# Neighborhood attention on one core: a rebuilt start, a new order of filler work, and a ring for the edge columns

## The chip, the core and the metric

The kernel runs on one core of a Trainium2 chip. The metric is the device time of one execution in microseconds. The engines are TensorE (PE; PEld is its weight load), VectorE (DVE), ScalarE (ACT), GpSimd (POOL) and SyncE (SP), which here only issues DMAs.

## The reference

Every pixel of a 224 x 224 image with 192 channels attends to a 7 x 7 neighborhood with dilation 2, clipped at the border; one head, all 192 channels.

```python
qkv = x @ wqkv                                 # q, k, v of 192 channels
r0 = jnp.clip(ir - 6, 0, H - 1 - 12); c0 = jnp.clip(ic - 6, 0, W - 1 - 12)
nidx = (r0 + 2*a) * W + (c0 + 2*b)             # a, b = 0..6: 49 neighbors
logits = jnp.einsum('bnc,bnkc->bnk', q, k[nidx]) * C ** -0.5
o = jnp.einsum('bnk,bnkc->bnc', softmax(logits), v[nidx]) @ wo
```

## The kernel before

Dilation 2 splits the keys by the parity of rows (rc) and of columns (cc). A step (rc, j) handles eight query rows of each column parity; j runs to 14, so there are 28 steps. In a step, order lists eight ticks: four for cc 0 and four for cc 1, each with three or four key tiles n of 8 rows x 8 columns from two neighboring key blocks, 128 keys.

Weights are folded. AW holds q times k weights, so that g = AW x is scored against raw x; WP folds v and output weights. The tile xt[b] is the block of 16 image rows with channels on partitions; XN[rc] has pixels on partitions, and between its channel columns stands a field of group columns (one-hot), from which the softmax sum comes. XA and XB are the key operands, copied from xt (key_items: "first" on GpSimd, "second" on VectorE), with one-hot key rows and columns in the spare rows of XB; GB carries the mask in the same rows on the query side.

In each tick s_stage (L364) does the score matmuls and ScalarE the exp; y_stage (L388) of the tick before multiplies the probabilities with XN; y_evac (L407) copies a finished half of y to SBUF, one tile on ScalarE and one on VectorE. Between them filler items are popped from one list: g_piece (L315), six a step, which makes the query side for the next step, and o_item (L419), seven a step, which makes the output of the step before: four matmuls, a reciprocal and a multiplication on VectorE. Both use the PSUM pool ps_go, which has two buffers. The list goes g, o, g, o, ... The g_piece of kind 1 is copied by VectorE (L333) and ScalarE (L334).

Near the image's left and right edge the clipped windows need other rows: gather_edges (L279) copies six columns of xt on GpSimd, edge_item multiplies them, and g_edges (L338) puts the results into g's first columns with eight small GpSimd copies a step, at tick 0 of the step before.

All instructions run on each engine in the order in which the program writes them (manual_schedule, L55). The loads of XN for later steps are divided between GpSimd's queue (nine tiles) and SP's (five); SP also issues the transposing load of xt (load_xt, L63, at tick 1 of a step with rc 0) and the stores of a finished step (store, L436).

The start (L472 to L521) loads both halves of XN, from SP, GpSimd and, behind the AW products, ScalarE (L486). It turns two blocks into xt with 84 TensorE transposes (L500), copied by ScalarE and VectorE, then makes keys, edges and the six g pieces of step 0, spreads masks and one-hot rows by DMA inside SBUF, and last makes the value weights.

Of the kernel before, what the change touches and what calls it, by code (L numbers as in the profile page):

```python
# [26 lines left out]
def kernel(  # L27
# [45 lines left out]
    nc.scalar.dma_start(out=w_lo[:], in_=wqkv[0:128, :])  # L73
    nc.scalar.dma_start(out=w_hi[:], in_=wqkv[128:192, :])
    nc.scalar.dma_start(out=wo_lo[:], in_=wo[0:128, :])
    nc.scalar.dma_start(out=wo_hi[:], in_=wo[128:192, :])

# [6 lines left out]
    def xn_items(rc, m, eng):  # L84
        if not (0 <= m < NJ):
            return []
        res = []
        r0, p0 = 16 * m + rc, (m % 2) * 64
        for n in range(NT):
            def one(n=n):  # L90
                eng.dma_start(out=XN[rc][p0:p0 + 64, XP * n + 64:XP * (n + 1)],  # L91
                              in_=xp[r0: r0 + 15: 2, TW * n: TW * (n + 1), :])
            res.append(one)
        return res
# [4 lines left out]

    run(xn_items(0, 0, nc.sync))  # L100
    run(xn_items(0, 1, nc.gpsimd))
    run(xn_items(1, 0, nc.sync))
# [4 lines left out]
    def turn_weights(X):  # L107
        for (dt_, d0, dn) in ((wT_lo, 0, 128), (wT_hi, 128, 64)):
            tp = ps_y.tile([128, 2, 128], BF, name="tp_w", tag="y")
# [8 lines left out]
    for nm in wnames:  # L118
        AW[nm] = const.tile([128, 128], BF, name="aw_" + nm)
        nc.vector.memset(AW[nm][:], 0.0)  # L120
# [9 lines left out]
    def make_aw():  # L130
        for k_, (reg, us) in enumerate(uses.items()):
# [5 lines left out]
            for (nm, o0, o1, d0) in us:  # L137
                nc.scalar.mul(AW[nm][rows, d0:d0 + o1 - o0], pt[rows, o0:o1], scale)
# [5 lines left out]

    def make_wp():
        for (cc, kt, c0, cn, p0) in ((0, 0, 64, 128, 0), (0, 1, 0, 64, 64), (1, 0, 0, 128, 0), (1, 1, 128, 64, 0)):
            pt = ps_y.tile([128, 512], F32, name="prW", tag="y")
            nc.tensor.matmul(pt[p0:p0 + cn, 0:C], lhsT=wT_lo[:, 2, c0:c0 + cn], rhs=wo_lo[:], start=True, stop=False)
            nc.tensor.matmul(pt[p0:p0 + cn, 0:C], lhsT=wT_hi[:, 2, c0:c0 + cn], rhs=wo_hi[:], start=False, stop=True)
            nc.scalar.copy(out=WP[p0:p0 + cn, cc, kt, 0:C], in_=pt[p0:p0 + cn, 0:C])  # L150

# [101 lines left out]
    def fill_groups(rc):  # L253
        t = XN[rc]
        nc.gpsimd.tensor_copy(out=t[:, 0:NT * XP].rearrange("p (n c) -> p n c", c=XP)[:, :, 0:64],
                              in_=grp[:].unsqueeze(1).to_broadcast([128, NT, 64]))
        nc.gpsimd.tensor_copy(out=t[:, NT * XP:], in_=grp[:])

# [19 lines left out]
    ge = {}  # L278
# [8 lines left out]
    def edge_item(b):  # L287
# [27 lines left out]
    def g_piece(rc, j, kind, ra):  # L315
# [5 lines left out]
        for (r0, n_, b, l0) in step_rows(rc, j):  # L321
# [5 lines left out]
            for i, (w, k) in enumerate(ws):  # L327
                nc.tensor.matmul(pg[:, a_ - ra:b_ - ra, p0:p0 + S - 3], lhsT=AW[w][:], rhs=xt[b][:, k, la:lb:2, p0:p0 + S - 3],  # L328
# [35 lines left out]
    def s_stage(st, cc, ns):  # L364
# [15 lines left out]
        nc.scalar.activation(out=G.p[:, 0:off], in_=s_ps[:, 0:off], func=ACTF.Exp)  # L380
# [7 lines left out]
    def y_stage(G):  # L388
        st, cc = G.st, G.cc
        xn = XN[st.rc]  # L390
        for (n, a, b, off) in G.sub:
            c0 = XP * n + (128 if cc == 0 else 256)
            c1 = XP * n + (0 if cc == 0 else 384)
            w = b - a
            pv = G.p[:, off:off + BR * w].rearrange("p (r c) -> p r c", c=w)
            for h in range(2):
# [5 lines left out]
                for kt, l0 in ((0, c0), (1, c1)):  # L402
                    nc.tensor.matmul(ys[kt][:, :, a_ - h0:b_ - h0], lhsT=xn[:, l0:l0 + 128], rhs=pv[:, :, a_ - a:b_ - a],  # L403
# [14 lines left out]

    def o_item(st, t):  # L419
        if t == 0:  # L420
            st.o = work.tile([128, NO, 2, C], BF, name="o_all", tag="o_all", bufs=2)
        po = ps_go.tile([128, 2, 256], F32, name="po", tag="go")
        for cc in range(2):
            for kt in range(2):
                nc.tensor.matmul(po[:, cc, 0:C + 1], lhsT=st.ysb[cc][:, kt, t, :], rhs=WP[:, cc, kt, :], start=(kt == 0), stop=(kt == 1))  # L425
        rs = work.tile([128, 2, 1], F32, name="rs", tag="rs", bufs=4)
        nc.vector.reciprocal(out=rs[:], in_=po[:, :, C:C + 1])  # L427
        if st is steps[-1]:
            nc.vector.tensor_scalar(out=st.o[:, t, 0, :], in0=po[:, 0, 0:C], scalar1=rs[:, 0, :], scalar2=None, op0=ALU.mult)
            nc.scalar.mul(st.o[:, t, 1, :], po[:, 1, 0:C], rs[:, 1, :])  # L430
        else:
            nc.vector.tensor_tensor(out=st.o[:, t], in0=po[:, :, 0:C], in1=rs[:].to_broadcast([128, 2, C]), op=ALU.mult)  # L432
        if t == NO - 1:
            store(st)

    def store(st):  # L436
        o = st.o
        runs = _affine([16 * b + l0 + 2 * i for (r0, n_, b, l0) in step_rows(st.rc, st.j) for i in range(n_)])
        last = st is steps[-1]
        for k, (i0, n_, d0, stp) in enumerate(runs):  # L440
# [6 lines left out]
            else:  # L447
                e = slice(NI * i0, NI * (i0 + n_ - 1) + 1, NI)
                for i in range(n_):
                    p0 = NI * (i0 + i)  # L450
                    (nc.sync, nc.scalar)[i % 2 if last else 0].dma_start(
                        out=op[d0 + i * stp, NO - 3:S - 3, :].rearrange("(i t) c -> i (t c)", t=NO),
                        in_=o[p0 + 1:p0 + NI].rearrange("p t two c -> p (t two c)"))
            q = nc.scalar if last and k else nc.sync
            q.dma_start(out=op[dr, NO - 4, :], in_=o[e, NO - 1].rearrange("p two c -> p (two c)"))
            q.dma_start(out=op[dr, 0:3, C:2 * C], in_=o[e, 0:3, 0, :])
            q.dma_start(out=op[dr, 0:3, 0:C], in_=o[e, 3:6, 0, :])
            q.dma_start(out=out[0][dr, W - 6:W, :], in_=o[e, 0:6, 1, :])
# [3 lines left out]
    last_of = {(0, 1): [(0, 0)], (0, 3): [(0, 1)], (1, 6): [(1, 1)], (1, 7): [(1, 0)]}  # L462
# [13 lines left out]
    cols_iota(1)  # L476
    make_groups()
# [3 lines left out]
    onehot_keys()  # L481
    mask_cols(1)
    turn_weights(0)
    turn_weights(1)
    make_aw()
    run(xn_items(1, 1, nc.scalar))  # L486
    spread_rows(nc.sync, 0, 1)
    spread_keys(nc.sync, 1, 0)
    fill_groups(0)
    fill_groups(1)  # L490
    for b in range(2):
        new_xt(b)
    for rc in range(2):
        for k in range(3):
            for h in range(2):
                hn = NT // 2
                tp = ps_y.tile([128, hn, 2, BR, TW], BF, name="tp_x", tag="y")
                for n in range(hn):
                    c0 = XP * (hn * h + n) + 64 + 128 * k
                    nc.tensor.transpose(tp[:, n].rearrange("p b r c -> p (b r c)"), XN[rc][:, c0:c0 + 128], ident[:])  # L500
                for b in range(2):
                    (nc.scalar.copy if b == h else nc.vector.tensor_copy)(  # L502
                        out=xt[b][:, k, rc:16:2, HALF * h:HALF * h + HALF].rearrange("p r (n c) -> p n r c", c=TW), in_=tp[:, :, b])
        ki = [key_items(b, rc) for b in range(2)]
        for i in range(4):
            ki[0][i]()
            ki[1][i]()
    for b in range(2):
        gather_edges(b)
        edge_item(b)  # L510
    run(g_items(0, 0))
    g_edges(0, 0)
    for gi in range(1, NG):
        mask_row(gi)
    spread_cols(nc.sync, 0)
    spread_keys(nc.sync, 0, 1)
    spread_cols(nc.sync, 1)
    spread_rows(nc.sync, 1, NG)
    spread_keys(nc.sync, 1, 1)
    turn_weights(2)  # L520
    make_wp()  # L521
# [3 lines left out]
    for si, st in enumerate(steps):  # L525
        st.ysb = [work.tile([128, 2, NO, 128], BF, name=f"ysb{cc}", tag=f"ysb{cc}", bufs=2) for cc in range(2)]
        nx = steps[si + 1] if si + 1 < len(steps) else None
        g_q = g_items(nx.rc, nx.j) if nx else []
        if si > 1:
# [3 lines left out]
        fill = []  # L533
        while g_q or o_q:
            fill += g_q[:1] + o_q[:1]
            g_q, o_q = g_q[1:], o_q[1:]
        fill = fill[::-1]
        for ti, (cc, ns) in enumerate(order):
            G = s_stage(st, cc, ns)
            if ti == 0 and nx:  # L540
                g_edges(nx.rc, nx.j)
            if fill and (ti > 0 or nx):
                fill.pop()()
            if prev is not None:
                y_stage(prev)
                for key in last_of.get((prev.cc, prev.tick), []):
                    y_evac(prev.st, *key)
# [10 lines left out]
            if fill and len(fill) >= len(order) - 1 - ti:  # L558
                fill.pop()()
            if ti == 4 and st.rc == 1:  # L560
                gather_edges(st.j + 2)
# [59 lines left out]
```

## Time and profile before

| | us |
|---|---|
| median of 3 runs | 422.8 (422.27 to 423.28) |
| profiled execution | 426.73 |
| its span | 424.8 |
| PE busy | 342.4 (81%) |
| DVE busy | 277.0 (65%) |
| ACT busy | 250.0 (59%) |
| POOL busy | 245.7 (58%) |

The span runs from the first to the last instruction of the profiled execution; its time has something around the span. Busy shares are means over the start, the middle and the end.

### The profile page before, as it was taken

The numbers are of one execution on the slowest core, as the hardware profiler recorded it, in microseconds if no ns is written. First come the engines' busy times: TensorE is split into PE (matmuls) and PEld (weight loads), VectorE is DVE, ScalarE is ACT, GpSimd is POOL, SyncE is SP. The second block draws the span as 40 slices with busy tenths as digits, with TensorE's granted clock in tenths as the row PEclk, the third lists the DMA queues.
The fourth block names the chain that finished last, engine by engine and source line by source line (L and its number), as shares of the span: only waits on it lengthen the run. The fifth ranks groups of instructions, "written<-read, shape, count | busy, mean of one in ns | idle before, by whom it ended". The sixth has DMA issues, their size and how long they took to land.

```text
span 424.8 us, 12956 instructions
## 1 busy us (share of the span) xinstructions
PE 342.4 (81%) x5012; PEld 288.5 (68%) x5012; DVE 277.0 (65%) x680; ACT 250.0 (59%) x557; POOL 245.7 (58%) x567
## 2 busy tenths in 40 slices
PE   5233899877898889998889878898898889898970
PEld 2123478766777778777778757787777778777850
DVE  2617437664777777676777657777777777777770
ACT  5023486662767666667666656666666575767650
POOL 9416500843885757776658866757858675790000
PEclk9999999996999999999999999999999999999996
DMA  5350090494895959979595995969869597542223
GB/s 148 104 140 3 2 178 2 108 167 120 168 203 125 170 155 189 159 147 188 154 175 143 153 192 137 168 148 194 179 134 174 160 159 167 141 128 72 66 67 65
DMA packets 96723, 57.86 MB, mean 136 GB/s; under 512 B 78134, under 2 KB 91270, under 8 KB 96662
## 3 DMA queue, kind: packets, MB, share of 16 engines
q1 hardware_dynamic: 84025, 44.42, 53.4%
q0 software_dynamic: 11040, 11.38, 12.6%
q10 hardware_dynamic: 1597, 1.24, 1.1%
q8 instruction: 39, 0.64, 0.7%
q14 instruction: 22, 0.18, 0.1%
HBM read 19.56 MB, written 19.27 MB: 91 GB/s over the span
## 4 chain that ended last, share of the span: by engine, by line
PE 44%; DVE 19%; ACT 18%; DMA 8%; issue 4%; SPq 3%; POOL 1%; ACTq 0%; DVEq 0%; POOLq 0%
PE pg L328 15%; PE po L425 10%; PE y L403 8%; DVE gbt L333 7%; ACT gbt L334 6%; DVE o_all L432 6%; DMA xn<-in_x_dram 6%; PE s_ps L376 5%; ACT p_sb L380 5%; PE s_ps L375 4%; ACT ysb L417 3%; SPq L91 2%; ACT ga L331 2%; DVE xb L272 2%; DVE rs L427 1%
## 5 line engine op out<-in xcount | busy, mean ns | idle before, releaser
L380 ACT ACTIVATE p_sb<-s_ps 128x448 bf16<-128x448 f32 x224 | 109.6, 489 | 87.9 <-PE s_ps L376 69.2
L91 POOL DMA_DIRECT2D xn<-in_x_dram x230 | 127.8, 592 | 35.6 <-PE y L403 21.3
L425 PE MATMUL po<-WP,ysb 128*128 128x193 bf16 x784 | 104.4, 250 | 23.2 <-ACT ysb L417 18.6
L403 PE MATMUL y<-p_sb,xn 128*128 128x112 bf16 (+2 forms) x1736 | 113.7, 207 | 7.8 <-DMA xn<-in_x_dram 7.1
L403 PEld LDWEIGHTS <-xn 128*128 128x128 bf16 x1736 | 97.9, 98 | 27.1 <-DMA xn<-in_x_dram 8.2
L432 DVE TENSOR_TENSOR o_all<-po,rs 128x384 bf16<-128x384 f32 x189 | 105.4, 558 | 8.4 <-DVE rs L427 0.2
L375 PE MATMUL s_ps<-ga,xa 128*128 128x112 bf16 (+2 forms) x812 | 104.4, 211 | 0.0
L376 PE MATMUL s_ps<-gbt,xb 128*128 128x112 bf16 (+2 forms) x812 | 101.9, 211 | 1.8 <-DVE xb L272 0.2
L425 PEld LDWEIGHTS <-ysb 128*128 128x128 bf16 x784 | 59.3, 98 | 34.2 <-ACT ysb L417 24.5
L376 PEld LDWEIGHTS <-xb 128*128 128x128 bf16 x812 | 77.3, 98 | 4.1 <-DVE xb L272 3.9
L417 DVE CAST ysb<-y 128x448 bf16<-128x448 f32 x104 | 64.0, 616 | 21.9 <-PE y L403 21.0
L375 PEld LDWEIGHTS <-xa 128*128 128x128 bf16 x812 | 77.7, 98 | 0.4 <-issue 0.4
L427 DVE RECIPROCAL rs<-po 128x2 f32<-128x2 f32 x196 | 32.6, 166 | 63.8 <-PE po L425 60.3
L268 POOL COPY xa<-xt 128x896 bf16<-128x896 bf16 x56 | 52.0, 977 | 17.8 <-DVE xt L502 17.8
L345 POOL COPY ga<-ge 128x9 bf16<-128x9 bf16 (+1 forms) x112 | 28.5, 276 | 53.6 <-DVE ge L301 50.2
L417 ACT CAST ysb<-y 128x448 bf16<-128x448 f32 x104 | 56.1, 540 | 0.6
L334 ACT CAST gbt<-pg 64x424 bf16<-64x424 f32 x56 | 28.4, 507 | 37.6 <-DVE gbt L333 37.6
L333 DVE CAST gbt<-pg 64x436 bf16<-64x436 f32 x56 | 33.8, 603 | 15.5 <-PE pg L328 14.7
L328 PE MATMUL pg<-xt,aw_m 128*128 128x327 bf16 (+2 forms) x252 | 42.5, 298 | 0.0
L328 PE MATMUL pg<-xt,aw_o 128*128 128x109 bf16 (+2 forms) x168 | 30.4, 290 | 10.7 <-ACT gbt L334 8.0
L331 ACT CAST ga<-pg 128x436 bf16<-128x436 f32 x56 | 29.4, 525 | 5.5 <-PE pg L328 5.5
L345 POOL COPY gbt<-ge 64x9 bf16<-64x9 bf16 (+1 forms) x112 | 29.9, 267 | 3.2
(91 smaller groups left out, 267.7 us busy)
## 6 DMA issues: line engine op xcount, KB each, us to landing
out_dram<-o_all SPq DMA_DIRECT2D x26, 630.0 KB
xn<-in_x_dram POOLq DMA_DIRECT2D x230, 48.0 KB, 4.4
xn<-in_x_dram SPq DMA_DIRECT2D x148, 48.0 KB
out_dram<-o_all SPq DMA_DIRECT2D x13, 78.8 KB
gbt<-gbt SPq DMA_DIRECT2D x3, 280.0 KB
out_dram<-o_all SPq DMA_DIRECT2D x52, 9.0 KB
xn<-in_x_dram ACTq DMA_DIRECT2D x14, 48.0 KB
xb<-xb SPq DMA_DIRECT2D x3, 224.0 KB
```

Source lines behind the costliest of these rows:

```text
L91: eng.dma_start(out=XN[rc][p0:p0 + 64, XP * n + 64:XP * (n + 1)], in_=xp[r0: r0 + 15: 2, TW * n: TW * (n + 1), :])
L328: nc.tensor.matmul(pg[:, a_ - ra:b_ - ra, p0:p0 + S - 3], lhsT=AW[w][:], rhs=xt[b][:, k, la:lb:2, p0:p0 + S - 3], start=(i == 0), stop=(i ...
L333: nc.vector.tensor_copy(out=Bt[0][0:64, ra:rb, 3:S], in_=pg[0:64, :, 0:S - 3])
L334: nc.scalar.copy(out=Bt[1][64:128, ra:rb, 6:S], in_=pg[64:128, :, 3:S - 3])
L345: nc.gpsimd.tensor_copy(out=dst.rearrange("p r s -> p s r"), in_=src)
L375: nc.tensor.matmul(o, lhsT=XA[:, cc, st.rc, n, :], rhs=A[cc][:, :, a:b], start=True, stop=False)
L376: nc.tensor.matmul(o, lhsT=XB[:, cc, st.rc, n, :], rhs=Bt[cc][:, :, a:b], start=False, stop=True)
L380: nc.scalar.activation(out=G.p[:, 0:off], in_=s_ps[:, 0:off], func=ACTF.Exp)
L403: nc.tensor.matmul(ys[kt][:, :, a_ - h0:b_ - h0], lhsT=xn[:, l0:l0 + 128], rhs=pv[:, :, a_ - a:b_ - a], start=not ys[2 + kt], stop=True, s ...
L417: eng(out=dst, in_=src.rearrange("p r i t -> p t i r"))
L425: nc.tensor.matmul(po[:, cc, 0:C + 1], lhsT=st.ysb[cc][:, kt, t, :], rhs=WP[:, cc, kt, :], start=(kt == 0), stop=(kt == 1))
L432: nc.vector.tensor_tensor(out=st.o[:, t], in0=po[:, :, 0:C], in1=rs[:].to_broadcast([128, 2, C]), op=ALU.mult)
```

## The change

Start: the four weight loads are written further down. Only the first key block is loaded at once (rc 0 from SP, rc 1 from GpSimd), and load_xt(1) stands behind it on SP. The transposes take 64 partitions and fill xt[0] alone, left half first; they now stand ahead of the mask work. Step 0 uses 64 keys (kp) and starts with other tiles (first_order); the two g pieces of kind 2, the keys of rc 1, the value weights and the second edge item become its filler. The second block's XN of rc 1 is loaded by SP. Group columns are written by VectorE, twice per tile (XP 448 to 512). Half of the AW scalings go to VectorE, and seven matmuls on constant data ("warm") are written in.

Steps: the list becomes g, g, o, o, g, o, o, ...; surplus items are popped later; SP's list of loads is emptied ahead of load_xt; edge_item moves to tick 1 of a step with rc 0, g_edges to tick 3, gather_edges to the end of a step with rc 1. The edge results lie in two rings of 24 rows (one per row parity), so that a step's rows are mostly one run of copies.

End: the last step's outputs of cc 0 are made within it, two tiles at a time (o_pair), those of cc 1 behind it in four buffers, on VectorE and ScalarE in turn; its stores go over three queues.

```diff
-XP = 448
+XP = 512
-    run(xn_items(0, 1, nc.gpsimd))
-    run(xn_items(1, 0, nc.sync))
+    run(xn_items(1, 0, nc.gpsimd))
+    load_xt(1)
...
+    ge = [const.tile([128, 15, NE], BF, name=f"ge{cl}") for cl in range(2)]      # NE = 3 * BR
+        for cl in range(2):                                       # edge_item
+            for (i, p, n_) in ring_runs(cl, BR * b, BR):
+                nc.vector.tensor_copy(out=ge[cl][:, :, p:p + n_], in_=pg[:, :, 2 * i + cl:2 * (i + n_ - 1) + cl + 1:2])
...
+    def o_pair(st, cc, t, pool, tag, k):
+        n_ = min(2, NO - t)
+        po = pool.tile([128, 2, 256], F32, name="po", tag=tag)
+        for i in range(n_):
+            o_mm(po[:, i, 0:C + 1], st, cc, t + i)
+        nc.vector.reciprocal(out=rs[:, 0:n_], in_=po[:, 0:n_, C:C + 1])
+        if k % 2 == 0:
+            nc.vector.tensor_tensor(out=st.o[:, t:t + n_, cc, :], ...)
+        else:
+            for i in range(n_):
+                nc.scalar.mul(st.o[:, t + i, cc, :], po[:, i, 0:C], rs[:, i, :])
...
+    new_xt(0)
+    for h in range(2):
+        for rc in range(2):
+            for k in range(3):
+                for n in range(hn):
+                    nc.tensor.transpose(..., XN[rc][0:64, c0:c0 + 128], ident[0:64, 0:64])
+                (nc.vector.tensor_copy if h == 0 and (k + rc) % 2 else nc.scalar.copy)(out=xt[0][...], in_=tp[:])
+    make_groups() ... onehot_keys(); fill_groups(0)
+    run(k00[0:2]); gather_edges(0)
+    g_piece(0, 0, 0, 0); g_piece(0, 0, 1, 0); g_piece(0, 0, 0, 4)
+    warm(4); g_piece(0, 0, 1, 4); warm(3)
+    edge_item(0); g_edges(0, 0)
...
+        return [lambda: g_piece(0, 0, 2, 0), lambda: g_piece(0, 0, 2, 4), f4, fw] + wp + g1[:3] + [f6] + g1[3:]
...
+            fill = g_q[:2]
+            if nx is None:
+                o_q += [(lambda k=k: o_pair(st, 0, 2 * k, ps_go, "go", 0)) for k in range((NO + 1) // 2)]
+            while g_q or o_q:
+                fill += o_q[:2] + g_q[:1]
...
             if ti == 1 and st.rc == 0:
+                run(sp_q)
+                sp_q = []
                 load_xt(st.j + 2)
...
-            if fill and len(fill) >= len(order) - 1 - ti:
+            if si > 0 and st.rc == 0 and ti == 1 and st.j + 1 < NJ:
+                edge_item(st.j + 1)
+            if si > 0 and ti == 3 and nx:
+                g_edges(nx.rc, nx.j)
+            if fill and (len(fill) >= nt - ti or (nx is None and ti < 4)):
                 fill.pop(0)()
```

## Rows read from the trace of the kernel before

**Rows 1.** The page, busy us, share of the span and instructions of the engines:

```profile
PE 342.4 (81%) x5012; PEld 288.5 (68%) x5012; DVE 277.0 (65%) x680; ACT 250.0 (59%) x557; POOL 245.7 (58%) x567
```

**Rows 2.** Windows: stretch, its us, busy us of each engine, granted clock, DMA share, GB/s:

```profile
28.00:52.20 24.20, 15.58 (x113) 10.71 (x113) 14.40 (x29) 9.94 (x24) 14.54 (x36) 0.98 0.07 17
...
150.00:200.00 50.00, 45.08 (x693) 38.64 (x692) 36.48 (x91) 32.84 (x72) 35.29 (x79) 1.00 0.88 165
```

**Rows 3.** Timeline of the start: start us, us, engine, line, operation [idle before, releaser]:

```profile
0.74 18.28 SPq L91 DMA_DIRECT2D xn<-in_x_dram  x28
...
9.89 0.28 DVE L251 TENSOR_SCALAR grp<-gi__189 128x64 bf16<-128x64 f32 x1 [6.81 <-POOL gi__189 L247]
...
11.74 2.34 PE L500 MATMUL tp_x<-ident,xn 128*128 128x128 bf16 x17 [0.42 <-DMA xn<-in_x_dram]
...
14.81 12.39 ACTq L91 DMA_DIRECT2D xn<-in_x_dram  x14
15.41 1.09 DVE L194 COPY xb<-t_r 32x1792 bf16<-32x1792 bf16 x1
...
27.24 0.53 ACT L502 COPY xt<-tp_x 128x448 bf16<-128x448 bf16 x1 [17.37 <-DMA gbt<-gbt]
...
48.94 2.78 DVE L230 CAST gbt<-rm 32x896 bf16<-32x896 f32 x5
...
52.20 0.28 PE L375 MATMUL s_ps<-ga,xa 128*128 128x112 bf16 x1
```

**Rows 4.** Timeline of ScalarE: first exps of steps 1 and 27, one same tick two steps apart:

```profile
62.62 0.54 ACT L380 ACTIVATE p_sb<-s_ps 128x448 bf16<-128x448 f32 x1
...
146.83 0.45 ACT L380 ACTIVATE p_sb<-s_ps 128x336 bf16<-128x336 f32 x1 [0.79 <-PE s_ps L376]
...
172.09 0.45 ACT L380 ACTIVATE p_sb<-s_ps 128x336 bf16<-128x336 f32 x1 [0.79 <-PE s_ps L376]
...
399.20 0.56 ACT L380 ACTIVATE p_sb<-s_ps 128x448 bf16<-128x448 f32 x1
```

**Rows 5.** Timeline of one step, from 385.98 us, TensorE's waits and a g evacuation:

```profile
388.39 0.34 PE L425 MATMUL po<-WP,ysb 128*128 128x193 bf16 x2 [0.71 <-ACT ysb L417]
...
389.62 0.60 DVE L333 CAST gbt<-pg 64x436 bf16<-64x436 f32 x1
...
390.26 0.51 ACT L334 CAST gbt<-pg 64x424 bf16<-64x424 f32 x1 [0.69 <-DVE gbt L333]
...
395.77 0.54 PE L328 MATMUL pg<-xt,aw_o 128*128 128x109 bf16 x4 [0.33 <-ACT gbt L334]
```

**Rows 6.** The page, costliest groups: busy us, mean ns, idle before and its releaser:

```profile
L432 DVE TENSOR_TENSOR o_all<-po,rs 128x384 bf16<-128x384 f32 x189 | 105.4, 558 | 8.4 <-DVE rs L427 0.2
...
L427 DVE RECIPROCAL rs<-po 128x2 f32<-128x2 f32 x196 | 32.6, 166 | 63.8 <-PE po L425 60.3
...
L417 ACT CAST ysb<-y 128x448 bf16<-128x448 f32 x104 | 56.1, 540 | 0.6
```

**Rows 7.** Timeline, TensorE's two long waits for x tiles:

```profile
98.31 0.37 PE L403 MATMUL y<-p_sb,xn 128*128 128x112 bf16 x2 [4.59 <-DMA xn<-in_x_dram]
...
253.40 0.27 PE L403 MATMUL y<-p_sb,xn 128*128 128x112 bf16 x2 [1.78 <-DMA xn<-in_x_dram]
```

**Rows 8.** Timeline of SP's queue over two steps:

```profile
110.38 7.83 SPq L66 DMA_TRANSPOSE xt<-in_x_dram  x1
118.31 3.46 SPq L91 DMA_DIRECT2D xn<-in_x_dram  x5
...
126.42 3.46 SPq L91 DMA_DIRECT2D xn<-in_x_dram  x5
131.02 0.92 SPq L445 DMA_DIRECT2D out_dram<-o_all  x1
```

**Rows 9.** Timeline of the end: the last normalization and the last stores:

```profile
415.15 0.42 ACT L430 ACTIVATE o_all<-po,rs 128x192 bf16<-128x192 f32 x1 [0.84 <-DVE o_all L429]
...
420.36 1.13 SPq L451 DMA_DIRECT2D out_dram<-o_all  x2
```

More of the change, by code (lines that the diff above doesn't have):

```diff
@@ L117 @@
     AW = {}
[L118 to L120 removed]
+    aw = const.tile([128, len(wnames), 128], BF, name="aw")
+    nc.vector.memset(aw[:], 0.0)
+    for i_, nm in enumerate(wnames):
+        AW[nm] = aw[:, i_, :]
     LO, HI = (0, 128, 0), (128, 64, 0)
@@ L476 @@
     cols_iota(1)
+    turn_weights(0, ps_y, "y")
+    turn_weights(1, ps_y, "y")
+    make_aw()
+    new_xt(0)
+    hn = NT // 2
+    for h in range(2):
+        for rc in range(2):
+            for k in range(3):
+                tp = ps_y.tile([128, hn, BR, TW], BF, name="tp_x", tag="y")
+                for n in range(hn):
+                    c0 = XP * (hn * h + n) + 128 + 128 * k
+                    nc.tensor.transpose(tp[:, n].rearrange("p r c -> p (r c)"), XN[rc][0:64, c0:c0 + 128], ident[0:64, 0:64])
+                (nc.vector.tensor_copy if h == 0 and (k + rc) % 2 else nc.scalar.copy)(
+                    out=xt[0][:, k, rc:16:2, HALF * h:HALF * h + HALF].rearrange("p r (n c) -> p n r c", c=TW), in_=tp[:])
     make_groups()
@@ L481, with warm @@
     onehot_keys()
+    fill_groups(0)
+    k00, k01 = key_items(0, 0), key_items(0, 1)
+    run(k00[0:2])
+    gather_edges(0)
+    wu = ps_s.tile([128, 512], F32, name="wu", tag="s")
+    def warm(n):
+        for _ in range(n):
+            nc.tensor.matmul(wu[:], lhsT=ident[:], rhs=w_lo[:, 0:512], start=True, stop=True)
+    g_piece(0, 0, 0, 0)
+    g_piece(0, 0, 1, 0)
+    g_piece(0, 0, 0, 4)
+    warm(4)
+    g_piece(0, 0, 1, 4)
+    warm(3)
+    edge_item(0)
+    g_edges(0, 0)
+    run(k00[2:3])
@@ L482 @@
     mask_cols(1)
[L483 to L486, printed above, removed]
+    run(k00[3:4])
     spread_rows(nc.sync, 0, 1)
     spread_keys(nc.sync, 1, 0)
[L489 to L507, printed above, removed]
@@ L523, with last_ticks @@
+    def last_ticks(od):
+        res = {}
+        for ti, (cc, ns) in enumerate(od):
+            for n in ns:
+                for (a, b) in pieces(cc, n):
+                    for h in range(2):
+                        if a < HALF * (h + 1) and b > HALF * h:
+                            res[(cc, h)] = ti
+        return res
     prev = None
@@ L532 @@
             pool_q += key_items(st.j + 1, 1 - st.rc)
[L533 to L538, printed above, removed]
+        nt = len(order)
+        for ti, (cc, ns) in enumerate(st.od):
             G = s_stage(st, cc, ns)
[L540 to L543, printed above, removed]
+            if fill and (nx or 0 < ti < 4 or ti > 5):
+                fill.pop(0)()
             if prev is not None:
                 y_stage(prev)
-                for key in last_of.get((prev.cc, prev.tick), []):
-                    y_evac(prev.st, *key)
+                for key, t_ in prev.st.last.items():
+                    if key[0] == prev.cc and t_ == prev.tick:
+                        y_evac(prev.st, *key)
             G.tick = ti
@@ L572 @@
     y_evac(prev.st, 1, 0)
-    run(o_q)
+    for k in range((NO + 1) // 2):
+        o_pair(prev.st, 1, 2 * k, *((ps_go, "go") if k % 2 == 0 else (ps_s, "s")), k)
+    store(prev.st)
 def _affine(vals):
```

163 lines of the change are left out of this document (97 added, 66 removed).

## Prediction

> **What bounds the kernel now.** I read the shares of the page first, then the stretches, then the timeline of the start, one step of the middle, the waits on loads, SP's queue and the end. TensorE is busy 81% of the span [rows 1], but the kernel has three parts with different limits. In the middle (150 to 200 us) it is busy 45.08 of 50 us; between 28.0 and 52.2 us, before the first score matmul, only 15.58 of 24.2 [rows 2].
>
> The start takes 52.2 us [rows 3]. The reader is to see there that the ScalarE queue issues 14 x loads from 14.81 to 27.20, and that ScalarE's first copy of a transposed block comes right behind, at 27.24; the 17 transposes from 11.74 on show that the x tiles of both halves had landed by then. So 13 us go to an engine that issues loads while work waits for it, and after it 48 copies, two blocks' keys, edges and weights are done one behind the other.
>
> In the middle a pair of steps lasts 172.09 - 146.83 = 25.26 us, 12.63 a step [rows 4]. From the first exp of step 1 (62.62) to that of the last (399.20) are 336.6 us for 26 steps, 8.2 more than 26 x 12.63 = 328.4. Two stalls on x loads make that up: 4.59 us seen by TensorE at 98.31 and 1.78 at 253.40 [rows 7]. Inside a step TensorE waits for evacuations [rows 5]: 0.71 us at the first output tile for ScalarE's copy of y, and 0.33 at an "o" piece of g for the chain VectorE 0.60, then ScalarE 0.51, which must follow since the second waits for the first. The period is regular, so this chain of small waits sets it, not the DMA share of 0.88 [rows 2]; SP, though, is nearly full (below).
>
> **The sum.** Made against the profiled execution: span 424.8 us, its time 426.73; the median of the timed runs, 422.8, lies 3.93 below that time, so I subtract 3.93 at the end.
>
> **The start, first score matmul.** Removed: the ScalarE loads, half of the x block (the first step uses 64 keys), half of the copies (12 for 24), the second block's keys. The second block now comes by a transposing load on SP, behind 14 loads of x. SP issued 28 loads in 18.28 us, 0.65 each [rows 3], so 14 end at 9.9 and land at about 12.5 as before. PE's 84 transposes now have 64 columns; bounds are the 0.138 of the row at 11.74 (2.34 / 17) and half of it, 6 to 12 us; I take 8, because ScalarE's copies pace them: 9 copies at 0.53 [rows 3], six of them behind the last landing, end at about 16.7. Meanwhile VectorE has its three copies until 12.9 and then the masks and one-hot keys, which took 9.89 to 16.50 = 6.6 us [rows 3]; now behind, they end at 19.5. Filling the group columns moves from GpSimd to VectorE; VectorE has no such row, bounds are 0 (hidden) and two copies of the GBT size, 2.78 / 5 = 0.56 each [rows 3]; I take 0.9 and the key copy 0.4: 20.8. The g pieces then need VectorE 0.60 and ScalarE 0.51 twice in turn [rows 5], with about 1 us of matmul between: 23.4, and an edge item behind it. First score matmul at 24, against 52.2: 28.2 less. Bounds: 20 (PE and copies alone) to 34 (the transposing load, 7.83 us of SP [rows 8], takes the DMA engines from the x tiles, and everything slides by up to 10).
>
> The 16 small memsets made into one, the extra AW scalings on VectorE, the 128-column group field (XP 512), the 64-row operands of the first step and the longer queue of weight loads cost nothing on this path: VectorE is idle between 3 and 9.9 us and the matmul's length is its columns. If that cover were gone it would be about 1 us.
>
> **Step 0.** Moved into it: two g pieces, eight key copies, the value weights, the second edge item, and behind them on VectorE the five mask rows (2.78 us [rows 3]). Before, 52.2 to about 62.3 was 10.1 us; VectorE starts it with some 6 us of leftovers, so I take 13.4. On SP stand the 14 x loads (9 us), then the five spreads, which end at about 32 and land before step 1 begins at 37.4. Step 1 was at 62.3: 24.9 less in all, bounds 16 to 30.
>
> **The 26 steps.** The fill order changes from g,o,g,o to g,g,o,o,g,o,o,g,o,o,g,o,g, and the surplus pieces come later. I laid one step out queue by queue with durations from the trace [rows 5, 6] (a normalization is 0.17 + 0.56 on VectorE, a y copy 0.54 on ScalarE and about 0.62 on VectorE). What goes: the first output tile stands a tick later, the two g pieces no longer queue behind each other's chain. What comes instead: ScalarE enters a step 1.2 us late, because it still has the exp, a g copy and a y copy of tick 7; then exp, g copy, y copy (0.54 + 0.52 + 0.54) put the first output tile at 2.9 us, a wait of 0.8 where it was 0.71. Behind g1 the next exp waits for VectorE and ScalarE; later the fourth g piece waits 0.3 for the output tile two before it (two PSUM buffers), the fifth 0.2, and the exp of tick 6 stands behind a ScalarE copy that waits for VectorE: 0.2 to 0.5. That sums to 12.13. In every second step the edge item sits in tick 1 with two or more VectorE copies in place of one, +0.64: 12.77. Mean 12.45, 0.18 less a step. The eight edge copies of GpSimd become about four; GpSimd is off the path, so nothing. Ends: all these waits gone [rows 5], 12.63 - 0.71 - 2 x 0.33 = 11.3 (SP forbids it, below), and 13.3, every wait kept and the edge's 0.64 on top. Sum: 26 x 0.18 = 4.7 less.
>
> **The two stalls.** The loads that were late stood on SP behind the transposing load (110.38, then 118.31) [rows 8]. The change empties SP's list of loads before it issues that one, so they come 7.8 us earlier; what is late next is the stores, which nobody waits for, and the gather of the next block's edges, now put at the end of a step. I count 8.2 less.
>
> **The last step and the end.** Its output tiles and four new pairs of cc 0 ride in the last step; the cc 1 pairs go in four buffers and turn about on two engines. Last step: 11 items at 0.73 of VectorE plus four y copies make about 13 us where it had 9.3; behind it 3.9 instead of 7.7. Nothing gained: the last normalization ends 16.4 us after 399.20 [rows 4, 9] and would do so again. The stores go over three queues, 6, 6 and 4 in place of 9 and 7, at about 0.7 each: 1.5 less.
>
> 24.9 + 4.7 + 8.2 + 1.5 = 39.3; 426.7 - 39.3 - 3.9 = 383.5. I say 384.
>
> [...] SP's transposing load takes 7.83 us of issue in the row, while its block of 16 rows has 1.38 MB [rows 8]. [...]
>
> **Rivals.** SP's work for two steps [rows 8] is one transposing load 7.83, ten loads 6.9 and two stores of some 4.6 each, 24.0 in 25.25; between 129.9 and 131.02 it is idle.
>
> B: the evacuations are less late than I lay them out and steps shrink to SP's floor, 12.0. For it: waits of over 1.3 us a step [rows 5]. Against: ScalarE and VectorE are in order. 26 x 0.45 = 11.7 less: 372.
>
> C: SP is the bound as it is; steps stay at 12.63, and SP, now 10 us of loads and spreads behind at the start, lets loads be late again. For: SP's rows touch each other. Against: the 1.1 us. 4.7 + 8.2 lost: 397. [...]
>
> D: the start shrinks less, since the transposing load and the x tiles fight for the DMA engines: first matmul at 34. For: only 0.07 of DMA share stood in the 28 to 52 stretch [rows 2], now it is all at once. 394.
>
> E, the other side: slower. The chain VectorE 0.60, ScalarE 0.51 with its hand-overs, 1.39 us, is uncovered three times a step, because pairs of pieces of one kind meet two PSUM buffers and each exp stands behind a copy that waits for VectorE. Three such waits in place of three shorter ones [rows 5] (0.71 + 2 x 0.33 = 1.37) give 12.63 + 4.17 - 1.37 = 15.4 a step, 26 x 2.98 = 77 more: 461. It decides from 12.45 + 39.3 / 26 = 13.96 a step on. Against it: between two such pieces stand 1.0 us or more of other matmuls.
>
> **How the numbers follow.** Forecast (374 to 394 alone) 0.45, B 0.20, C 0.16, D 0.12, E 0.07. The range takes in B, C, D and half a microsecond a step to both sides, 364 to 401, and leaves out E and what is beyond B. What a measurement of this kernel can tell from no change is about 0.2%, 0.8 us. Only E is slower: 0.06 slower, 0.01 the same, 0.93 faster.
>
> **What would show it.** First score matmul at 20 to 28 us; ScalarE's first transposed copy before 12; step 1 at 34 to 42; pairs of steps of 24.9, one step about 0.6 longer than the next; no wait on x loads above 1 us; first store 16 to 17 us after the last step's first exp. Wrong: a first matmul past 34, a pair below 24 or above 26, or a wait on a load that comes back.

## The result

The changed kernel takes 371.16 us (median of 12 runs, 369.44 to 384.08); the kernel before, beside it, 424.35 (15 runs). The ratio is 0.8745, 95% interval 0.8717 to 0.8774. Ratios, here and below, leave out executions in a slower state (of these 12 the two at 376.46 and 384.08), while medians are of all. I had said 384, 364 to 401: right in sign and inside the range, but the gain is 53 us and not 39, and it does not sit where I put it. By the prediction's own list of signs one came that it called wrong: a pair of steps below 24 us. The profiled execution took 371.12, its span is 369.3.

Page of the changed kernel, busy us of the engines (compare [rows 1]):

```profile
PE 337.0 (91%) x5018; PEld 285.3 (77%) x5019; DVE 275.8 (75%) x693; ACT 239.1 (65%) x542; POOL 233.6 (63%) x472
```

Windows of the changed kernel, columns as in [rows 2]:

```profile
28.00:52.20 24.20, 19.59 (x248) 14.69 (x247) 16.16 (x36) 12.36 (x28) 13.28 (x25) 0.86 0.66 144
...
150.00:200.00 50.00, 48.83 (x753) 41.66 (x750) 40.00 (x101) 35.97 (x81) 35.81 (x70) 1.00 0.78 177
```

TensorE's work is nearly the same (337.0 us against 342.4); in the middle it now fills 48.83 of 50 us, where it filled 45.08. Two places are worse than the rest: the stretch above that holds step 0 (granted clock 0.86), and step 4, from 76 to 94 us (below).

Timeline of the start, changed kernel (compare [rows 3]):

```profile
10.33 5.68 SPq L66 DMA_TRANSPOSE xt<-in_x_dram  x1
...
13.10 2.34 PE L526 MATMUL tp_x<-ident,xn 64*128 64x64 bf16 x37 [0.88 <-DMA xn<-in_x_dram]
...
13.61 2.71 ACT L527 COPY xt<-tp_x 128x448 bf16<-128x448 bf16 x6 [1.92 <-PE tp_x L526]
...
21.46 0.24 PE L394 MATMUL s_ps<-ga,xa 128*64 128x112 bf16 x1
```

The first score matmul comes at 21.46 instead of 52.20. A transpose of 64 columns takes 2.34 / 37 = 0.063 us, a little under half of the 0.138 before, and the six copies behind the last landing end at 16.3.

Timeline of ScalarE, exps: the first of step 1, one same tick two steps apart, the first of step 27 (compare [rows 4]):

```profile
41.93 0.55 ACT L399 ACTIVATE p_sb<-s_ps 128x448 bf16<-128x448 f32 x1
...
205.62 0.45 ACT L399 ACTIVATE p_sb<-s_ps 128x336 bf16<-128x336 f32 x1 [0.20 <-PE s_ps L395]
...
228.66 0.45 ACT L399 ACTIVATE p_sb<-s_ps 128x336 bf16<-128x336 f32 x1 [0.20 <-PE s_ps L395]
...
346.93 0.56 ACT L399 ACTIVATE p_sb<-s_ps 128x448 bf16<-128x448 f32 x1
```

A pair of steps takes 23.04 us, 11.52 a step, against 25.26. Step 0 is 20.5 us long (from the first score matmul at 21.46 to the first exp of step 1 at 41.93), against 10.4.

Timeline of one step, changed kernel (compare [rows 5]); the first row is the step's first score matmul:

```profile
208.62 0.21 PE L394 MATMUL s_ps<-ga,xa 128*128 128x112 bf16 x1
...
209.28 0.56 ACT L399 ACTIVATE p_sb<-s_ps 128x448 bf16<-128x448 f32 x1
...
209.72 0.54 ACT L342 CAST ga<-pg 128x436 bf16<-128x436 f32 x1
...
210.12 0.57 ACT L436 CAST ysb<-y 128x448 bf16<-128x448 f32 x1
...
210.55 0.54 PE L440 MATMUL po<-WP,ysb 128*128 128x193 bf16 x4
...
211.65 0.50 PE L440 MATMUL po<-WP,ysb 128*128 128x193 bf16 x4 [0.17 <-ACT gbt L345]
...
214.03 0.56 DVE L453 TENSOR_TENSOR o_all<-po,rs 128x384 bf16<-128x384 f32 x1
214.50 0.16 DVE L452 RECIPROCAL rs<-po 128x2 f32<-128x2 f32 x1
```

The first output tile, at 210.55, has no bracket: TensorE does not wait where it waited 0.71. What the starts show: 209.28, 209.72, 210.12. Instructions of 0.56 and 0.54 us follow each other at 0.44 and 0.40, because a row's last 0.12 to 0.14 lies beside the next one. VectorE does the same: 0.56 at 214.03, the next at 214.50, 0.09 beside each other.

Timeline of the one stall that is left, in step 4 (compare [rows 7]):

```profile
79.94 0.83 POOL L296 COPY xe<-xt 128x144 bf16<-128x144 bf16 x2 [7.37 <-DMA xt<-in_x_dram]
...
80.44 0.74 PE L305 MATMUL pe<-xe,aw 128*128 128x48 bf16 x12 [1.97 <-POOL xe L296]
...
82.65 0.56 DVE L453 TENSOR_TENSOR o_all<-po,rs 128x384 bf16<-128x384 f32 x1 [4.37 <-DMA out_dram<-o_all]
...
83.27 0.83 PE L440 MATMUL po<-WP,ysb 128*128 128x193 bf16 x4 [2.08 <-DVE o_all L453]
```

Step 4 takes 17.9 us instead of 11.7. The edge copies of GpSimd wait for the x block, VectorE waits for a store to free its output tile. TensorE's two waits are 4.0 us; the other 2.2 come behind them, where the granted clock is lower: four output matmuls take 0.83 where they take 0.50 to 0.54 at clock 1.00. The same comes in step 0, behind a wait of 4.39 us that ends at 35.37. Windows of the changed kernel, the stretches behind the two waits (the granted clock is the third number from the end):

```profile
35.37:40.70 5.33, 5.33 (x48) 3.46 (x48) 1.08 (x3) 2.23 (x5) 3.98 (x10) 0.54 1.23 268
...
83.27:88.29 5.02, 5.02 (x44) 4.46 (x45) 2.78 (x10) 1.91 (x4) 4.90 (x11) 0.52 0.74 211
```

Both are a little over half; before the waits (28 to 31 and 76 to 78.4 us), and from 40.70 and 88.29 on, it is 1.00. Each stretch is full of TensorE's work, so at clock 1.00 it would be some 2.4 us shorter (an estimate: 5.33 x 0.46 and 5.02 x 0.48).

The x block and the stores that step 4 waits for both go through SP's queue. SP's timeline of the changed kernel, one load ahead of step 4 and two in the middle (compare [rows 8]):

```profile
65.88 7.96 SPq L66 DMA_TRANSPOSE xt<-in_x_dram  x1
...
204.83 5.42 SPq L66 DMA_TRANSPOSE xt<-in_x_dram  x1
...
214.98 3.41 SPq L86 DMA_DIRECT2D xn<-in_x_dram  x5
219.44 0.91 SPq L481 DMA_DIRECT2D out_dram<-o_all  x1
...
227.81 5.89 SPq L66 DMA_TRANSPOSE xt<-in_x_dram  x1
```

In the middle the transposing load takes 5.4 to 5.9 us and not 7.83, and SP is idle 1.05 us from 218.39 to 219.44; ahead of step 4 it takes 7.96.

The end, timeline of ScalarE and of its queue (compare [rows 9]):

```profile
360.65 1.15 ACT L469 ACTIVATE o_all<-po,rs 128x192 bf16<-128x192 f32 x3 [1.65 <-DVE rs L464]
...
366.54 0.73 ACTq L494 DMA_DIRECT2D out_dram<-o_all  x1
```

The last normalization ends 14.9 us after 346.93 (16.4 before), the span 7.5 after that (9.2 before).

### The profile page after: what moved, and what is told of

It reads as the page before. It is cut to its first block, busy times and chain, and to the rows that moved or that the text cites. A ratio compares the mean times of both kernels' runs of the same rounds, so it can differ in the third digit from the quotient of the medians.

```text
span 369.3 us, 12812 instructions
## 1 busy us (share of the span) xinstructions
PE 337.0 (91%) x5018; PEld 285.3 (77%) x5019; DVE 275.8 (75%) x693; ACT 239.1 (65%) x542; POOL 233.6 (63%) x472
## 4 chain that ended last, share of the span: by engine, by line
PE 63%; DVE 21%; ACT 6%; DMA 3%; issue 2%; SPq 2%; POOL 0%; POOLq 0%; DVEq 0%; ACTq 0%
PE pg L339 18%; PE y L422 15%; PE po L440 12%; DVE ysb L436 8%; PE s_ps L394 8%; PE s_ps L395 8%; DVE o_all L453 4%; DVE gbt L344 4%; ACT gbt L345 4%; PE pe L305 2%; DVE gbt L234 2%; DMA out_dram<-o_all 1%; DMA w_hi<-in_wqkv_dram 1%; DMA xn<-in_x_dram 1%; SPq L86 1%
## 5 line engine op out<-in xcount | busy, mean ns | idle before, releaser
L399 ACT ACTIVATE p_sb<-s_ps 128x448 bf16<-128x448 f32 (+1 forms) x224 | 106.8, 489 | 39.3 <-PE s_ps L395 37.8
L422 PE MATMUL y<-p_sb,xn 128*128 128x112 bf16 (+3 forms) x1736 | 113.0, 208 | 0.1
L422 PEld LDWEIGHTS <-xn 128*128 128x128 bf16 (+1 forms) x1736 | 98.8, 98 | 16.7 <-issue 6.9
L339 PE MATMUL pg<-xt,aw 128*128 128x436 bf16 (+2 forms) x588 | 104.1, 296 | 2.0
L394 PE MATMUL s_ps<-ga,xa 128*128 128x112 bf16 (+3 forms) x812 | 103.5, 211 | 0.0
L395 PE MATMUL s_ps<-gbt,xb 128*128 128x112 bf16 (+3 forms) x812 | 102.0, 211 | 0.0
L394 PEld LDWEIGHTS <-xa 128*128 128x128 bf16 (+1 forms) x812 | 77.9, 99 | 4.6 <-issue 1.3
L395 PEld LDWEIGHTS <-xb 128*128 128x128 bf16 (+1 forms) x812 | 78.1, 99 | 2.9
L436 DVE CAST ysb<-y 128x448 bf16<-128x448 f32 x104 | 64.7, 622 | 20.9 <-PE y L422 17.9
L345 ACT CAST gbt<-pg 64x424 bf16<-64x424 f32 x56 | 28.4, 507 | 49.5 <-DVE gbt L344 49.5
L339 PEld LDWEIGHTS <-aw 128*128 128x128 bf16 x588 | 42.4, 100 | 17.3 <-DVE o_all L453 5.9
L362 POOL COPY ga<-ge 128x24 bf16<-128x24 bf16 (+5 forms) x60 | 21.0, 358 | 16.4 <-DVE ge L313 11.0
L347 ACT CAST ga<-pg 128x424 bf16<-128x424 f32 x56 | 28.6, 513 | 0.1
```

The costliest lines, as they stand in the source:

```text
L345: nc.scalar.copy(out=Bt[1][64:128, ra:rb, 6:S], in_=pg[64:128, :, 3:S - 3])
L394: nc.tensor.matmul(o, lhsT=XA[:, cc, st.rc, n, G.kp], rhs=A[cc][:, :, a:b], start=True, stop=False)
L395: nc.tensor.matmul(o, lhsT=XB[:, cc, st.rc, n, G.kp], rhs=Bt[cc][:, :, a:b], start=False, stop=True)
L399: nc.scalar.activation(out=G.p[G.kp, 0:off], in_=s_ps[G.kp, 0:off], func=ACTF.Exp)
L422: nc.tensor.matmul(ys[kt][:, :, a_ - h0:b_ - h0], lhsT=xn[G.kp, l0:l0 + 128], rhs=pv[:, :, a_ - a:b_ - a], start=not ys[2 + kt], stop=True ...
L436: eng(out=dst, in_=src.rearrange("p r i t -> p t i r"))
```

## The experiments

**1. The list.** In the changed kernel, the old list and the old rule for surplus pieces in steps 1 to 26; and the other way round, the kernel before with the new list and rule alone. (The edits are shown cut.)

```
-            fill = g_q[:2] ...   fill += o_q[:2] + g_q[:1]
+            fill += g_q[:1] + o_q[:1]           (e1; e8 is the reverse, in the kernel before)
```

> The changed kernel with the old list of filler items (g,o,g,o) and the old rule for surplus items in steps 1 to 26; all else as changed. Theory L (the list shortens the steps, because the waits of the old period, 0.71 and twice 0.33 us, go): a pair of steps goes from 22.97 back to about 25 us, the time from 371 to 393 to 400. Rival P (the places of edge item, edge copies and loads shorten them): the pair stays near 23.0 and the time at 369 to 374.

> The kernel before with only the new list (g,g,o,o,g,...) and the new rule for surplus items in steps 1 to 26. Theory L: its pair of steps falls from 25.26 to 23 to 23.6, the time from 423 to 394 to 402 (the stalls on loads may grow, since SP has less time). Rival P: 25 and 418 to 424.

The changed kernel with the old list takes 401.93 us, ratio to before 0.949 (0.944 to 0.954); the kernel before with the new list 399.06, ratio 0.9407 (0.9352 to 0.9462). Timeline of TensorE with the old list:

```profile
211.91 0.34 PE L440 MATMUL po<-WP,ysb 128*128 128x193 bf16 x2 [0.71 <-ACT ysb L436]
...
232.62 0.53 PE L339 MATMUL pg<-xt,aw 128*128 128x436 bf16 x2 [0.34 <-ACT gbt L345]
...
237.81 0.34 PE L440 MATMUL po<-WP,ysb 128*128 128x193 bf16 x2 [0.71 <-ACT ysb L436]
```

The kernel before with the new list, its middle (windows); then two waits of TensorE (us in total, times, longest), first in the kernel before, then there with the new list:

```profile
150.00:200.00 50.00, 47.76 (x745) 41.43 (x743) 38.73 (x96) 34.89 (x78) 38.50 (x86) 1.00 0.85 181
```

```profile
PE po L425 <- ACT ysb L417: 18.6, 26, 0.7
PE pg L328 <- ACT gbt L334: 8.5, 25, 0.5
```

```profile
PE po L425 <- ACT ysb L417: 0.7, 1, 0.7
PE pg L328 <- ACT gbt L334: 0.5, 1, 0.5
```

The waits of [rows 5] (0.71, and 0.33 to 0.34) come back with the old list, and go with the new one in the old kernel. In the kernel before they come to 27.1 us in some 26 steps, 1.04 a step, near the 1.11 by which a step is shorter (12.63 to 11.52). The list alone is worth 25 to 31 us. With the old list SP had room (its transposing loads took 5.5 us in the median, and from step 7 on it was idle 2.8 to 4.5 us in each pair) and a pair still took 25.9 (211.91 to 237.81). And with the new list in the old kernel SP's rows touch nearly all along, yet a pair takes 23.4 in the mean of steps 6 to 23, and the transposing load 6.5 in the median where it took 7.8: SP was not what set 25.26.

**2. Edges at their old places.**

```
+            if si > 0 and ti == 0 and nx:  g_edges(nx.rc, nx.j)
+            if ti == 4 and st.rc == 1:  gather_edges(st.j + 2)
+            if ti == 6 and st.rc == 1 and st.j + 2 < NJ:  edge_item(st.j + 2)
```

> The changed kernel with gather, edge item and edge copies at their old places (ticks 4, 6 and 0). Theory L: the edge item costs TensorE and VectorE the same elsewhere, so the pair stays within 0.4 us of 22.97 and the time within 368 to 376. Rival P: the pair goes to 24.5 to 25.3, the time to 391 or more.

373.05, ratio 0.881 (0.8762 to 0.8859); steps of 11.2 and 11.8 us in turn, 23.0 a pair as in the changed kernel. The edges' places are not where the gain is.

**3. SP's list of loads not emptied ahead of the transposing load.**

```
-                run(sp_q)
-                sp_q = []
                 load_xt(st.j + 2)
```

> The changed kernel without emptying SP's list of loads ahead of the transposing load. My prediction's step (late loads stood behind that load): waits of TensorE on x tiles come back, 5 to 9 us in all, 376 to 380. Rival: the one stall left, at 79 to 83 us, has its own cause (stores and the transposed block), and the loads were in time anyway: 369 to 373.

374.61 (369.16, 372.45, 376.76 and 381.4), ratio 0.8751 (0.8673 to 0.8828), around the changed kernel's: four executions so far apart tell no gain of that edit. The one trace is of the execution of 381.4, and in it TensorE waits for x tiles (us in total, times, longest):

```profile
PE y L422 <- DMA xn<-in_x_dram: 12.1, 14, 3.1
```

The changed kernel's trace has no such wait. So loads can be late behind the transposing load, as I had said; what emptying the list is worth in a usual execution stays open.

**4. Step 0's masks.** Four of the five mask rows of VectorE in step 1.

```
-    for gi in range(1, NG):  mask_row(gi)
+    mask_row(1)              (the others: one a tick in step 1)
```

> The changed kernel with four of the five mask rows taken out of the start and written one a tick in step 1 (and the spread of the mask rows cut in two for it). Theory V: in step 0 TensorE waits 4.39 us for a g copy that stands behind VectorE's leftovers, 5.84 of them the mask rows, which GpSimd's key copies slow from 0.56 to 1.17 each. Without four of them step 0 is 3 to 5 us shorter, step 1 at most 1 longer: 366 to 369. Rival D (the spreads and key copies are late as well and hold step 1): no gain, 370 to 372.

370.54, ratio 0.874 (0.870 to 0.878): no difference that can be told. Its one trace is of an execution of 379.89 us, so where the gain of step 0 went in the five others (368.89 to 371.1) is not shown; with the stores moved too it stays (experiment 11).

**5. A third output tile.** It takes away what VectorE waits for at 82.65.

```
-  tag="o_all", bufs=2
+  tag="o_all", bufs=3
```

> The changed kernel with three output buffers in place of two. Theory S: the stall from 78 to 84 us is an output tile waiting for a buffer whose store is late on SP (VectorE waits 4.37 on a store, TensorE 2.1 on VectorE), so it goes: 2 to 5 us less, 366 to 369. Rival X: the transposed block lands at 79.9 whatever the buffers, TensorE still waits 1.97 for the gather and the stall only changes its name: 370 to 371.5.

A miss: 386.97, ratio 0.9119 (0.9071 to 0.9166), 16 us slower than with two. Its transposing load (source view: ns min/median/max) and its waits:

```profile
L66 SPq DMA_TRANSPOSE xt<-in_x_dram x13: 6060/7825/9692, 10.4 to 315.4; - x13
```

```profile
POOL xe L296 <- DMA xt<-in_x_dram: 73.2, 11, 8.3
...
PE pe L305 <- POOL xe L296: 16.5, 9, 3.7
```

The load's issue takes 7.8 in the median (5.9 in the changed kernel), SP's rows touch from 62 us to the last load but for two gaps of under 0.5, and GpSimd's edge copies wait for the block 11 times (once in the changed kernel), and TensorE for them 9 times.

**6. Step 0's sixteen stores on SP and GpSimd.**

```
-  qs = (nc.sync, nc.scalar, nc.gpsimd) if last else (nc.sync,)
+  qs = ... if last else (nc.sync, nc.gpsimd) if st is steps[0] else (nc.sync,)
```

> The changed kernel with the 16 stores of step 0 divided between SP and GpSimd. Theory S': SP is about 5 us behind from those 16 stores (52.15 to 62.2 us); with half of them gone the loads, the transposing load and the next stores come 4 to 5 us earlier and the stall at 78 to 84 goes, 4 to 6 us less, 365 to 367.5. Rival: GpSimd's queue, now later with its own x loads, stalls step 2 or 3: 370 or more.

369.64, ratio 0.8729 (0.8686 to 0.8773): no difference that can be told. The stall of step 4 is gone (11.7 us), but step 2 has one (14.7), since GpSimd's edge copies now stand behind its stores. TensorE there, timeline:

```profile
57.76 0.74 PE L305 MATMUL pe<-xe,aw 128*128 128x48 bf16 x12 [2.87 <-POOL xe L296]
```

**7. The seven warming matmuls left out.**

```
-    warm(4)
-    warm(3)
```

> The changed kernel without the seven matmuls on constant data. If they only fill TensorE's waits, first score matmul and time stay (21.5 us, 370.5 to 372). If they hold the granted clock, the first ticks of step 0 run at half of it: up to 2 us more, though step 0 waits for VectorE later on and would hide most of it.

371.01, ratio 0.876 (0.8722 to 0.8799): nothing in sum. The trace shows two effects, one each way: the first score matmul comes 1.2 us sooner, at 20.27, and from there to 25.5 the granted clock is 0.67 (I had said half), where the changed kernel has 1.00 from 21.46 to 26.7.

**8. Three tiles and two queues.** Edits 5 and 6 together.

> The changed kernel with three output tiles instead of two, and step 0's sixteen border stores on SP and GpSimd instead of on SP alone. With three tiles alone (386.97) SP was never idle from step 2 to the end and its transposing load took 6.8 to 9.7 us instead of 5.4 to 7.2. Theory Q (the third tile only lets the computing run on while SP is behind from step 0; once behind, SP's transposing load always runs beside GpSimd's loads and key copies and takes 8 us, so that SP needs 24.9 a pair and never catches up): without the pile of stores SP is not behind, the transposing loads take 5.3 to 7, edge copies do not wait for them, and the time is 365 to 371. Rival R (three tiles put more stores in flight, and those slow the loads whatever the start): pairs stay near 25 and the time is 381 to 388.

368.91, ratio 0.8721 (0.8677 to 0.8765), as with edit 6 alone. The third tile does no harm where SP is not behind from the start; the load takes 5.6 in the median and no edge copy waits for it:

```profile
L66 SPq DMA_TRANSPOSE xt<-in_x_dram x13: 5316/5609/6604, 10.0 to 297.8; - x13
```

**9. The same with one push:** three extra stores on SP behind step 12.

```
+        if si == 12:
+            for _ in range(3):  store(steps[si - 1])
```

> Three output tiles and step 0's stores on two queues (368.91), and at the end of step 12 three further stores of step 11's finished tile, the same bytes to the same place, some 14 us of SP's queue once. Theory Q (once SP is behind with three tiles it stays behind): up to step 12 pairs of 23.0 and transposing loads of 5.3 to 6.6 as without them; after it SP has no idle time, transposing loads of 7.5 to 8.5, edge copies of GpSimd waiting for them, and pairs of 24.5 to 25.3 to the end; 380 to 395. Rival C (SP catches up by its idle 1 to 2 us a pair): one late spell of up to 14 us or none, transposing loads back at 5.3 to 6.6 within three pairs, the last pairs 23.0; 369 to 379.

386.78, ratio 0.9053 (0.9005 to 0.9102). SP's loads either side of the push, and the waits:

```profile
180.50 5.45 SPq L66 DMA_TRANSPOSE xt<-in_x_dram  x1
...
217.48 7.76 SPq L66 DMA_TRANSPOSE xt<-in_x_dram  x1
```

```profile
POOL xe L296 <- DMA xt<-in_x_dram: 29.4, 5, 8.1
```

The push delays step 14 by 8.2 us (19.9 in place of 11.7, by the traces of experiments 8 and 9), and the steps behind it lose 10.1 more: the edge copies wait for all five later blocks, the transposing load stays at 6.7 to 8.3, and SP has no idle time to the last load. The pairs are uneven (22.6 to 28.2, 24.6 in the mean). Theory Q holds in the main: once SP was behind, it stayed behind for the rest of the kernel.

**10. Three tiles, stores on SP, without GpSimd's key copies** (the keys of blocks 2 to 13 are not made).

```
-            res += [first, second]
+            res += [first, second] if b < 2 else [second]
```

> Three output tiles, step 0's stores all on SP as in the changed kernel (this combination took 386.97), with GpSimd's key copies of blocks 2 to 13 left out (XA keeps the keys of blocks 0 and 1; VectorE's copies and all loads stay). Theory P (the transposing load takes 8 us in place of 5.4 because GpSimd works beside it, its copies about as much as its loads): the loads take 6 to 6.8, SP's work of a pair falls below 23.5, SP catches up within some pairs, and the time is 367 to 376. Rival T (only the transfers in flight stretch it, or GpSimd's loads alone): the loads stay at 7.4 to 8.5 and the time is 381 to 389.

383.89, ratio 0.8988 (0.8945 to 0.9031); theory P fell:

```profile
L66 SPq DMA_TRANSPOSE xt<-in_x_dram x13: 5192/7706/8452, 10.1 to 312.7; - x13
```

GpSimd's key copies are not what stretches the load. Whether its loads do, or the transfers in flight, stays open.

**11. A better start.** Edit 6; the third edge gather ahead of GpSimd's stores; mask rows 3 to 5 in steps 1 and 2; the second group fill behind two more g pieces.

```
-    for gi in range(1, NG):  mask_row(gi)      -    fill_groups(1)
+    mask_row(1);  mask_row(2)                  (fill_groups(1) behind g1[2])
+            if si == 1 and ti == 3:  gather_edges(2)
+            if (si, ti) in ((1, 5), (2, 4), (2, 5)):  mask_row(3 if si == 1 else ti)
```

> The changed kernel (two output tiles) with step 0's border stores on SP and GpSimd, the third edge gather of GpSimd put into the middle of step 1 (ahead of those stores on its queue), mask rows 3 to 5 moved to steps 1 and 2, and the group fill of the second half behind two more g pieces. Theory V (VectorE's leftovers of 10 us, slowed by GpSimd's key copies, make step 0 20 us long): step 0 lasts 15.5 to 17.5, step 1 about 12, step 2 below 12, and the time is 363 to 367. Rival (the start is bound by what GpSimd has to do, or the gain is given back in the next steps as with the masks alone, 370.5): 368 to 372.

365.03 (362.6 to 367.02), ratio 0.8622 (0.8579 to 0.8666): faster than both kernels. Step 0 takes 15.7 us (21.18 to 36.88, where it took 20.5) and step 4 11.8; no slice of its page but the last has a granted clock below 0.9. Steps 1 and 2 give 3 back (12.8 and 13.2, where I had said about 12 and below 12, and the changed kernel has 11.4 and 11.7). This puts three edits together; what each is worth alone beside the others is not shown.

## Why the prediction was right in range and wrong inside

By the profiled spans (424.8 and 369.3), forecast and measured, in us:

```
                                    said    measured
start to the first score matmul    -28.2     -30.7
step 0                              +3.3     +10.0
26 steps (13 pairs)                 -4.7     -28.9
stalls in them                      -8.2      -2.7
last step and normalizations         0        -1.5
stores                              -1.5      -1.7
sum                                -39.3     -55.5
```

**The start** was right to 2.5 us and in its working: 64-column transposes just under the lower bound, copies done at 16.3, VectorE's one-hot copies and the group fill as the last thing. Rival D (loads fighting) did not come: SP's first transposing load took 5.68, beside the x tiles. The 64-row operands cost next to nothing, as I had said: in the changed kernel's trace a matmul on 64 rows takes 217 ns in the mean with 112 columns, one on 128 rows 213, and the length does go by the columns (187 with 48, 357 with 436), though not in proportion.

**The 26 steps are the failed term**, 24 us too small. I wrote that "ScalarE enters a step 1.2 us late" and that "exp, g copy, y copy (0.54 + 0.52 + 0.54) put the first output tile at 2.9 us, a wait of 0.8". I added durations of rows end to end, though starts are 0.40 to 0.44 apart. In the step shown above, counted from its first score matmul (208.62), the exp starts at 0.66 where I had 1.2, and the first output tile at 1.93 where I had 2.9, and nothing waits. These 0.97 us are about what a step is shorter than forecast (12.45 - 11.52 = 0.93). Six ScalarE instructions that I had laid end to end (three of tick 7, three of the next tick) make up some 0.8 of them at 0.12 to 0.14 each, an estimate; no experiment tests it. The kernel before had these starts too, ScalarE's timeline:

```profile
386.94 0.54 ACT L380 ACTIVATE p_sb<-s_ps 128x448 bf16<-128x448 f32 x1 [0.19 <-PE s_ps L376]
387.38 0.52 ACT L331 CAST ga<-pg 128x436 bf16<-128x436 f32 x1
387.78 0.55 ACT L417 CAST ysb<-y 128x448 bf16<-128x448 f32 x1
```

What is left is TensorE's own work: 45.08 / 50 x 12.63 = 11.39 us a step from [rows 2, 4], the end of "all these waits gone" that I had put at 11.3 and excluded with "SP forbids it". It forbade nothing: 24.0 per pair was made of a 7.83 that shrinks to 5.4. Steps take 11.3 and 11.7 in turn, 0.4 apart, where I had 0.64 for the edge item.

**Step 0 is mis-sized the other way**, by 6.7: the time that TensorE waits for VectorE's leftovers, and the lower clock behind that wait, for which I had no term. I took [rows 3]'s 0.56 for a mask row and 0.40 for a key copy. Timeline of step 0, changed kernel:

```profile
23.80 5.84 DVE L234 CAST gbt<-rm 32x896 bf16<-32x896 f32 x5
...
23.91 6.52 POOL L273 COPY xa<-xt 128x896 bf16<-128x896 bf16 x5
...
31.49 1.58 DVE L277 COPY xb<-xt 64x896 bf16<-64x896 bf16 x4
...
34.18 0.59 DVE L344 CAST gbt<-pg 64x436 bf16<-64x436 f32 x1
...
35.37 0.66 PE L305 MATMUL pe<-xe,aw 128*128 128x48 bf16 x12 [4.39 <-ACT gbt L345]
```

Beside GpSimd's copies a mask row takes 5.84 / 5 = 1.17, and the g copy that TensorE waits for stands behind 10 us of such leftovers. TensorE's wait is 4.39, and the clock of 0.54 behind it costs some 2.4 more (the estimate above): together 6.8. In experiment 11, where step 0 is shorter, the granted clock of that stretch (31 to 37 us) is 0.9 or more by its page, and there it is the key copies' turn to be slow, same view:

```profile
25.58 4.11 DVE L277 COPY xb<-xt 64x896 bf16<-64x896 bf16 x4
```

1.03 each, where GpSimd is copying (its five key copies there run from 23.63 to 29.45), and 0.40 in the fence above, where it had done. GpSimd pays too, 6.52 / 5 = 1.30, where two of these copies take 1.84 in the middle of the kernel. So both sides are slower there: a key copy of VectorE that takes 0.40 and one of GpSimd that takes 0.92, together 1.32, come every 1.03 and 1.16 beside each other in experiment 11. Why is not shown. I had priced the copies as if alone.

**The stalls**: "what is late next is the stores, which nobody waits for" failed. VectorE waits for them as soon as it needs the output tile two steps on (4.37 us at 82.65). The other thing named there, the gather of the edges, was late too (1.97 us of TensorE at 80.44). Whether the emptied list gave what I had counted stays open (experiment 3).

**The last step** gained 1.5, where I had said nothing. Its sum has a slip: 11 items at 0.73 and four y copies at 0.62 are 10.5 and not 13, and by that the gain would have been 2.6. The stores were right.

**The rivals.** 371 is next to B's 372, but not by B: its floor of 12.0 a step did not exist. C's stuck queue is real in this kernel, though not in the traced execution of this version: experiments 5, 9 and 10 sit in it, at 384 to 387. In the kernel before SP's rows touch but for 1.1 us a pair, and experiment 1 shows that the list bound it all the same. D and E did not come.

The errors are 28.4 us one way (steps, start, last step, stores) and 12.2 the other (step 0, stalls), 16.2 of span. The 3.9 that I subtracted for the median were not there in the changed kernel (371.12 profiled, 371.16 median), which leaves 12.3. That the range held is in part their cancelling.

## What to carry to other kernels

For a chain of short instructions on one engine (0.4 to 0.6 us here), take the distance of the starts from the timeline and not the durations; and hold the period that comes out against the busy time that the busiest engine needs for it, which here was the answer. An engine that is full in the trace of before is a bound only if its rows keep their length: the rows of this issuing queue vary from 5 to 10 us, and it stayed full while a pair of steps fell by 1.8 us (experiment 1). Before moving work to an engine to shorten a start, see what its neighbour does at that time (a mask row took 1.17 us beside GpSimd's copies and 0.56 without them), and what is in order behind it. And where the forecast has TensorE wait for some microseconds, look at the granted clock behind such a wait (0.54 and 0.52 here) and give it a term.

## What the runs showed of the hardware

The same transposing load of 1.38 MB takes 5.2 us (experiment 10) to 10.1 (the kernel before) of SP's issue time. Its medians are 5.4 to 5.9 where SP is idle now and then (the changed kernel, experiments 8 and 11, the old list in experiment 1) and 7.7 to 7.8 where SP has next to no idle time (the kernel before, experiments 5 and 10), with values between, such as 6.5 in the kernel before with the new list; one push of three stores (experiment 9) took it from 5.45 to 6.7 and more for the rest of the kernel. Why the issue takes longer is not shown. A third output tile made this kernel slower (386.97 against 371.16, experiment 5): the wait that it removes (two tiles, step 4) was, as I read experiments 5 and 8, what let SP catch up. Behind waits of 4.39 us and of 1.97 and 2.08 close together the granted clock was 0.54 (35.37 to 40.70) and 0.52 (83.27 to 88.29), at a price of 2.2 to 2.5 us each, an estimate from what was left of step 4's length and from the two stretches.
